# Decode attention with grouped K/V heads: the first K block is loaded ahead of wq and x, and transposed ahead of the q projection

## Chip, cores, metric

One core of a Trainium2 chip (trn2), the other cores idle. The time is that of one execution on the device, in microseconds (us); most executions of one kernel agree within 0.3%. Runs are called fast or slow by their time against the fastest of the same kernel (slow is over 1.5% longer), and only fast runs are compared. The span in a profile is some 1.8 us shorter than the time.

## The reference

```python
B, Sq, D = 8, 4, 512
Hq, Hkv, Sk, Dh = 32, 8, 2048, 128        # bfloat16 throughout

q = (x @ wq).reshape(B, Sq, Hq, Dh).transpose(0, 2, 1, 3)
k = repeat(k_cache, 4, axis=1);  v = repeat(v_cache, 4, axis=1)
scores = einsum("bhqd,bhkd->bhqk", q, k) * Dh ** -0.5
o = einsum("bhqk,bhkd->bhqd", softmax(scores), v)
out = o.transpose(0, 2, 1, 3).reshape(B, Sq, Hq * Dh) @ wo
```

K and V are 33.5 MB each, wq and wo 4.2 MB each: 75.5 MB to read, for little arithmetic.

## The kernel before

The work is 32 units (4 pairs of K/V heads x 8 batches). A unit needs one K block and one V block of 1 MB each. All loads go out on one queue, in a fixed order, as buffers come free (7 for K, 6 for V):

```python
nc.sync.dma_start(wq_sb[:, :, :], wq.rearrange("(p r) n -> p r n", r=R))   # 4 MB
nc.sync.dma_start(x_sb[:, :], x.flatten_outer_dims())                       # 32 KB
loads = []
for u in range(NU + KA):                       # NU = 32 units, KA = 4
    if u < NU:
        loads.append(("k", u))
    if u >= KA - 1 and u - KA + 1 < NU:
        loads.append(("v", u - KA + 1))
    ...                                        # parts of wo at the end
load_ready(0, 0)                               # as many as there are buffers for
```

Then come x's transposes, the q projection (128 matmuls `psq`), the spreading of q into block-diagonal form (`pse`, `q_bd`), and the loop. A step of the loop is half a unit: K is turned by PE transposes in two parts (`kp`), evicted to `kt`, scores, exp, and, six steps behind, values and norms:

```python
for step in range(-L - 1, NH):                 # L = 6, NH = 64
    i, j = step + L + 1, step + L
    if i < NH:
        transpose_part(i, 0)                   # 4 transposes, 1 eviction
    if 0 <= j < NH:
        scores(j)
    if i < NH:
        transpose_part(i, 1)
    ...                                        # norms, values, finish of `step`
    load_ready(min((i + 1) // 2, NU), max((step + 1) // 2, 0))
```

After the loop 8 projection matmuls, the last permutation of the output and the last 32 projection matmuls remain. A free buffer is not all that a load waits for: it also waits for the eighth load before it to land (in the trace of before, the ninth load waited 8.6 us for wq).

The softmax here doesn't subtract the row's maximum and nothing guards it: scores larger than these inputs give would overflow.

## Time and profile before

| | before |
|---|---|
| time, median of 3 runs | 190.12 us (190.0 to 193.26) |
| the profiled run: time; span | 190.41 us; 188.6 us |
| read from HBM | 75.53 MB |
| rate once running | 424 GB/s |
| busy: PE, DVE, ACT | 82%, 60%, 46% |
| x landed; scores of unit 0 began | 13.58; 23.51 us |
| first V load that waited long for its buffer (block 6), issued | 39.58 us |
| last wait for wo ended; end | 181.98; 188.6 us |

How to read it: the row `GB/s` of the page gives the rate in 40 slices of the span, and whether the stream of loads is ever interrupted. The chain of waits goes back from the last instruction; a load in it has length "issue to landing", which is mostly standing in line when the line is long. The timeline of the issuing queue (`SPq`) tells when a load was put in line. The row of the granted clock, `PEclk`: `9` or 1.00 is full speed.

### The profile page before, as it was taken

To read this page: it belongs to the slowest core of one execution; us is meant where nothing else is said; L and a number is where in the kernel's file an instruction comes from. 1 tells how busy PE (TensorE), PEld (TensorE's weight loads), DVE (VectorE), ACT (ScalarE), POOL (GpSimd) and SP (SyncE) were. 2 spreads that over 40 slices of the span, in tenths; PEclk is the share of its full clock that TensorE was granted. 3 is DMA by queue.
4 is the path that set the end of the run, shared out by engine and by line. 5 is a ranking of instruction groups with operands and counts; after the bars stand their busy time and mean duration, and the time that the engine had idled before them with its cause. 6 is when DMAs were issued, how large, how long until landed. Compare 5 with 4: busy or idle time off the path is not lost.

```text
span 188.6 us, 6460 instructions
## 1 busy us (share of the span) xinstructions
PE 154.3 (82%) x2892; PEld 139.7 (74%) x2892; DVE 113.7 (60%) x220; ACT 86.3 (46%) x170; POOL 1.1 (1%) x8
## 2 busy tenths in 40 slices
PE   0009887899999999999888789998886899899783
PEld 0008677699999898898788788887776788787572
DVE  6401754577777677767766567676665677663420
ACT  2003456665655666446554354555554555542000
POOL 2000000000000000000000000000000000000000
PEclk9999999999999999999999999999999999999999
DMA  6999999999999999999999999999999999999950
GB/s 222 445 389 429 424 427 424 424 424 429 422 419 429 424 419 420 433 424 419 422 429 426 426 424 419 433 419 422 431 417 429 422 424 431 415 425 425 414 205 9
DMA packets 10539, 75.97 MB, mean 403 GB/s; under 512 B 1200, under 2 KB 1296, under 8 KB 1936
## 3 DMA queue, kind: packets, MB, share of 16 engines
q1 hardware_dynamic: 10464, 75.55, 95.7%
q8 instruction: 22, 0.36, 0.7%
q14 instruction: 5, 0.04, 0.1%
q10 hardware_dynamic: 48, 0.02, 0.0%
HBM read 75.53 MB, written 0.03 MB: 401 GB/s over the span
## 4 chain that ended last, share of the span: by engine, by line
DMA 80%; PE 12%; ACT 3%; DVE 2%; issue 1%; SPq 0%; DVEq 0%
DMA k_sb<-in_k_cache_dram 64%; DMA wo_sb<-in_wo_dram 9%; DMA x_sb<-in_x_dram 7%; PE kp L200 4%; PE s_ps L218 2%; PE psq L162 2%; PE out_ps L310 2%; ACT kt L205 2%; DVE kt L207 1%; PE o_ps L242 1%; ACT probs L228 1%; DVE q_bd L186 1%; PE pse L177 1%; PE l_ps L256 0%; ACT q_bd L186 0%
## 5 line engine op out<-in xcount | busy, mean ns | idle before, releaser
L200 PE MATMUL kp<-ident,k_sb 128*128 128x128 f32 x512 | 80.9, 284 | 9.3 <-DMA k_sb<-in_k_cache_dram 9.1
L207 DVE COPY kt<-kp 128x1024 bf16<-128x1024 bf16 x96 | 65.4, 684 | 25.4 <-PE kp L200 24.8
L228 ACT ACTIVATE probs<-s_ps 64x256 bf16<-64x256 f32 x128 | 48.4, 378 | 67.1 <-PE s_ps L218 66.4
L200 PEld LDWEIGHTS kp<-ident,k_sb 128*128 128x128 f32 x512 | 55.2, 142 | 10.6 <-issue 10.1
L218 PE MATMUL s_ps<-q_bd,kt 128*128 128x64 bf16 x1024 | 42.4, 194 | 3.1 <-ACT kt L205 2.6
L218 PEld LDWEIGHTS <-kt 128*128 128x128 bf16 x1024 | 39.8, 98 | 4.8 <-ACT kt L205 3.1
L242 PEld LDWEIGHTS <-v_sb 128*128 128x128 bf16 x1024 | 34.4, 96 | 9.3 <-DMA v_sb<-in_v_cache_dram 1.9
L264 DVE TENSOR_REDUCE l_sb<-l_ps 128x32 f32<-128x512 f32 x32 | 22.1, 692 | 23.5 <-PE l_ps L256 23.5
L242 PE MATMUL o_ps<-probs,v_sb 128*128 128x32 bf16 x1024 | 35.1, 176 | 0.9 <-DMA v_sb<-in_v_cache_dram 0.9
L205 ACT COPY kt<-kp 128x1024 bf16<-128x1024 bf16 x32 | 32.4, 1012 | 0.8
L256 PE MATMUL l_ps<-probs,ones 128*128 128x512 bf16 x64 | 19.1, 379 | 0.0
L268 DVE RECIPROCAL r_sb<-l_sb 128x32 f32<-128x32 f32 x32 | 11.3, 353 | 1.1
L153 PE MATMUL xtp<-ident,x_sb 32*128 32x32 bf16 x4 | 0.5, 191 | 13.9 <-DMA x_sb<-in_x_dram 13.6
L153 PEld LDWEIGHTS <-x_sb 32*128 32x128 bf16 x4 | 0.3, 114 | 13.9 <-DMA x_sb<-in_x_dram 13.6
L169 ACT ACTIVATE qT_all<-psq 128x256 bf16<-128x256 f32 x4 | 1.5, 385 | 15.0 <-PE psq L162 15.0
L310 PE MATMUL out_ps<-wo_sb,oP 128*32 128x256 bf16 x64 | 7.6, 272 | 0.8 <-DMA wo_sb<-in_wo_dram 0.8
L310 PEld LDWEIGHTS <-oP 128*32 128x32 bf16 x64 | 6.1, 96 | 1.5 <-issue 0.7
L363 ACT CAST out_sb<-out_ps 32x256 bf16<-32x256 f32 x1 | 0.4, 362 | 14.5 <-PE out_ps L310 14.5
L273 DVE TENSOR_TENSOR oT_all<-o_ps,r_sb 128x32 bf16<-128x32 f32 x32 | 5.8, 182 | 1.7 <-PE o_ps L242 1.5
L256 PEld LDWEIGHTS <-ones 128*128 128x128 bf16 x64 | 6.0, 98 | 0.8 <-issue 0.4
L186 DVE CAST q_bd<-pse 64x512 bf16<-64x512 f32 x4 | 2.6, 682 | 4.7 <-PE pse L177 4.7
L156 DVE COPY xT_sb<-xtp 128x32 bf16<-128x32 bf16 x4 | 0.5, 170 | 7.1 <-PE xtp L153 7.1
(23 smaller groups left out, 34.4 us busy)
## 6 DMA issues: line engine op xcount, KB each, us to landing
k_sb<-in_k_cache_dram SPq DMA_DIRECT2D x32, 1024.0 KB, 20.2
v_sb<-in_v_cache_dram SPq DMA_DIRECT2D x32, 1024.0 KB, 20.1
wq_sb<-in_wq_dram SPq DMA_DIRECT2D x1, 4096.0 KB, 12.6
wo_sb<-in_wo_dram SPq DMA_DIRECT2D x2, 1024.0 KB, 18.5
wo_sb<-in_wo_dram SPq DMA_DIRECT2D x3, 512.0 KB, 17.6
wo_sb<-in_wo_dram SPq DMA_DIRECT2D x2, 256.0 KB, 13.2
x_sb<-in_x_dram SPq DMA_DIRECT2D x1, 32.0 KB, 12.4
out_dram<-out_sb SPq DMA_DIRECT2D x1, 16.0 KB, 1.4
```

The lines of the kernel that those rows point to most:

```text
L186: (nc.scalar.copy if g else nc.vector.tensor_copy)(out=q_bd[rows, p, :, :, g, :], in_=pse[rows, :, :, :])
L200: nc.tensor.transpose(kp[:, j, :], k4[:, w : w + 128], ident4[:, :])
L205: nc.scalar.copy(out=kt2, in_=kp2)
L207: nc.vector.tensor_copy(out=kt2, in_=kp2)
L218: nc.tensor.matmul(s_ps[:, 2 * j : 2 * j + 2, :], lhsT=k_t[:, j % (HC // 4), :, e], rhs=q_bd[:, p, e, b, :, :], start=(e == 0), stop=(e == 1),
L228: nc.scalar.activation(out=pr[rows, hf * HC : (hf + 1) * HC, cols], in_=s_ps[rows, :, cols], func=EXP)
L242: nc.tensor.matmul(o_ps[u][:, :], lhsT=vs[u][:, cc, :], rhs=pr[:, cc, :], start=(cc == 0), stop=(cc == C - 1),)
L256: nc.tensor.matmul(l_ps[:, :, :], lhsT=ones[:, :], rhs=pr[:, c : c + LC, :], start=(c == 0), stop=(c + LC == C),)
L264: nc.vector.tensor_reduce(out=l_sb[:, :], in_=l_ps[:, :, :].rearrange("d c q -> d q c"), axis=AX, op=ADD)
L268: nc.vector.reciprocal(r_sb[:, :], l_sb[:, :])
L273: nc.vector.tensor_tensor(out=oT_all[:, p * HP : (p + 1) * HP, b, :], in0=o_ps[u][:, :].rearrange("d (h s) -> d h s", h=HP), in1=r_sbs[u][ ...
L310: nc.tensor.matmul(out_ps[half][:, :], lhsT=oP[p][:, r, :], rhs=wo_sb[:, p, r, half * DH : (half + 1) * DH], start=(p == 0 and r == 0), st ...
```

## The change

Its intent: PE sat idle until x arrived at 13.6 us, since wq and x are first in line. With K block 0 ahead of them, its 16 transposes can fill that idle time, and the scores can follow the q projection at once.

```diff
+    load_k(0)
     nc.sync.dma_start(wq_sb[:, :, :], wq.rearrange("(p r) n -> p r n", r=R))
     nc.sync.dma_start(x_sb[:, :], x.flatten_outer_dims())
     loads = []
     for u in range(NU + KA):
-        if u < NU:
+        if 0 < u < NU:
             loads.append(("k", u))
...
+    (kt and transpose_part are moved up to here, unchanged)
+    for i in range(2):
+        for part in range(2):
+            transpose_part(i, part)
     for r in range(R):
         xtp = psum_o.tile([128, T], BF16, tag="o", name="xtp")
...
     for step in range(-L - 1, NH):
         i, j = step + L + 1, step + L
-        if i < NH:
+        if 1 < i < NH:
             transpose_part(i, 0)
         if 0 <= j < NH:
             scores(j)
-        if i < NH:
+        if 1 < i < NH:
             transpose_part(i, 1)
```

More of the change, by code (lines that the diff above doesn't have):

```diff
@@ L149, with transpose_part @@
         nc.vector.memset(t[:, :, :], 0.0)
+    kt = {}
+    def transpose_part(i, part):
+        u, hf = divmod(i, 2)
+        c0 = hf * HC + part * (HC // 2)
+        kp = psum_k.tile([128, HC // 4, 128], FP32, tag="k", name="kp")
+        k4 = ks[u][:, :, :].rearrange("s c d -> s (c d)").bitcast(FP32)
+        for j in range(HC // 4):
+            w = (c0 // 2 + j) * 128
+            nc.tensor.transpose(kp[:, j, :], k4[:, w : w + 128], ident4[:, :])
+        kp2 = kp[:, :, :].rearrange("k j s -> k (j s)").bitcast(BF16)
+        k_t = ktpool.tile([128, HC // 4, 128, 2], BF16, tag="kt", name="kt")
+        kt2 = k_t[:, :, :, :].rearrange("k j s e -> k (j s e)")
+        if part == 1 and hf == 1:
+            nc.scalar.copy(out=kt2, in_=kp2)
+        else:
+            nc.vector.tensor_copy(out=kt2, in_=kp2)
+        kt[(i, part)] = k_t
+    for i in range(2):
+        for part in range(2):
+            transpose_part(i, part)
     for r in range(R):
@@ L190 @@
     wo_sb = wpool.tile([128, G2, WR, D], BF16, tag="w", name="wo_sb")
-    kt = {}
-    def transpose_part(i, part):
-        u, hf = divmod(i, 2)
-        c0 = hf * HC + part * (HC // 2)
-        kp = psum_k.tile([128, HC // 4, 128], FP32, tag="k", name="kp")
-        k4 = ks[u][:, :, :].rearrange("s c d -> s (c d)").bitcast(FP32)
-        for j in range(HC // 4):
-            w = (c0 // 2 + j) * 128
-            nc.tensor.transpose(kp[:, j, :], k4[:, w : w + 128], ident4[:, :])
-        kp2 = kp[:, :, :].rearrange("k j s -> k (j s)").bitcast(BF16)
-        k_t = ktpool.tile([128, HC // 4, 128, 2], BF16, tag="kt", name="kt")
-        kt2 = k_t[:, :, :, :].rearrange("k j s e -> k (j s e)")
-        if part == 1 and hf == 1:
-            nc.scalar.copy(out=kt2, in_=kp2)
-        else:
-            nc.vector.tensor_copy(out=kt2, in_=kp2)
-        kt[(i, part)] = k_t
     def scores(i):
```

## The prediction

> **What bounds the kernel now.** I read the page's slices first, then the windows by stage, then the chain that ended last, and then the timeline of the start and of the DMA-issuing queue. The slices of the page:
>
> ```profile
> PE   0009887899999999999888789998886899899783
> DMA  6999999999999999999999999999999999999950
> GB/s 222 445 389 429 424 427 424 424 424 429 422 419 429 424 419 420 433 424 419 422 429 426 426 424 419 433 419 422 431 417 429 422 424 431 415 425 425 414 205 9
> HBM read 75.53 MB, written 0.03 MB: 401 GB/s over the span
> ```
>
> The DMA row reads 9 from the second slice to the 38th. The rate settles at about 424 GB/s and stays there; only the first slice and the last two are low. The kernel must read 75.53 MB, and 75.53 MB / 424 GB/s = 178.1 us, of a span of 188.6 us. The other 10.5 us are the ramp at the start (some 2 us until the first bytes flow, plus a slow first slice) and the work after the last weights land. PE shows 9 in many slices as well, so I checked whether it or the stream sets the pace where both are full:
>
> ```profile
> 38.00:44.00 6.00, 6.00 (x125) 5.68 (x123) 4.60 (x11) 3.51 (x8) 0.00 (x0) 1.00 1.01 423
> 60.00:165.00 105.00, 93.62 (x1818) 86.19 (x1814) 71.97 (x137) 54.89 (x109) 0.00 (x0) 1.00 1.01 424
> ```
>
> In these window rows (length, busy PE, PEld, DVE, ACT, POOL, granted clock, DMA share, GB/s) PE is full between 38 and 44 us, catching up from its late start, yet the stream still moves 423 GB/s. So even where PE is behind, the stream does not slow. The chain that ended last (start, length, what):
>
> ```profile
> 1.18 12.40 DMA x_sb<-in_x_dram
> ...
> 14.55 3.57 PE psq L162 x126
> ...
> 21.15 2.56 PE kp L200 x12
> ...
> 43.70 0.33 SPq L103
> ...
> 44.08 19.80 DMA k_sb<-in_k_cache_dram
> ...
> 165.09 16.89 DMA wo_sb<-in_wo_dram
> ...
> 182.02 3.67 PE out_ps L310 x32
> ...
> 185.71 0.36 ACT out_sb L363
> ```
>
> The trap is its first 43.7 us. It runs through the load of x, the q projection, the transposes and the compute behind them, up to a V load that is issued at 43.70. Taken literally, everything that starts the compute earlier would end the kernel earlier. But the link from 44.08 to 63.88 is a 1 MB block that took 19.8 us to land; at 424 GB/s one takes 1.049 / 424 = 2.47 us. It spent 17.3 us in line behind other blocks. What counts is whether the line ever runs empty. The issuing queue answers that:
>
> ```profile
> 1.65 2.05 SPq L93 DMA_DIRECT2D k_sb<-in_k_cache_dram  x4
> ...
> 13.38 0.33 SPq L103 DMA_DIRECT2D v_sb<-in_v_cache_dram  x1
> ...
> 24.84 0.33 SPq L93 DMA_DIRECT2D k_sb<-in_k_cache_dram  x1
> ...
> 33.97 0.33 SPq L93 DMA_DIRECT2D k_sb<-in_k_cache_dram  x1
> 39.58 0.33 SPq L103 DMA_DIRECT2D v_sb<-in_v_cache_dram  x1
> ```
>
> The longest gap there after the start, from 33.97 to 39.58, is a V load that waits for its buffer, which PE releases late. By 39.58 the slices have moved (222+445+389+429+424+427+424+424) x 4.715 us = 15.01 MB by 37.7 us, and 1.9 us x 424 = 0.79 MB more: 15.8 MB. Less wq and x (4.22 MB) that is 11 blocks; 16 K and V blocks had been issued. Five were still in line, 12.3 us of transfer. That is the reserve at its thinnest.
>
> **What the Trainium skill says.** "DMA: Bandwidth & Descriptors", section "Bandwidth", gives 425 GB/s for a 16 MB load to 128 partitions on one core, and 435 as the fabric's ceiling; this trace's 424 agrees, so the stream has no speed left to gain. The same page, "Queues, rings and completion order", says that each of the 16 engines consumes its ring's descriptors in order. The trace agrees: x, 32 KB, issued at 1.18 behind 4 MB of wq, lands 12.40 us later, after wq (waited for until 13.38). So K block 0 placed first delays wq and x by its own transfer time. "Perfetto Trace Analysis", section "Identifying the Most-Contended Engine", says to improve the most-contended engine first; here that is the DMA, and the change takes no byte from it.
>
> **The change part by part.** The same 75.53 MB, instructions and buffers remain; the built order confirms that each engine keeps its instructions but for place (one kt copy of the first block is still on ACT, three on DVE).
>
> (a) K block 0 goes first. It lands at an estimated 4.5 us (first bytes at about 1.8, plus 2.47, plus a little). wq and x land 2.47 us later: x at 13.58 + 2.47 = 16.05 us.
>
> (b) The 16 transposes of block 0 leave the place after the q projection. By the rows
>
> ```profile
> 20.95 2.76 PE L200 MATMUL kp<-ident,k_sb 128*128 128x128 f32 x12
> 22.04 0.69 DVE L207 COPY kt<-kp 128x1024 bf16<-128x1024 bf16 x1 [0.17 <-PE kp L200]
> 25.17 1.01 ACT L205 COPY kt<-kp 128x1024 bf16<-128x1024 bf16 x1
> ```
>
> the first 12 cost 2.56 us of the chain, the last four 0.48. They move to about 4.5 to 8.5 us, where PE has nothing to do. DVE is clearing probs until 6.94 us, so the first copy comes then: 6.94 + 3 x 0.69 = 9.0 us for the three, ACT's by about 9.2, all before x lands. Three PSUM buffers mean that the fourth group waits for the first copy; that is hidden too.
>
> (c) The q path shifts whole by 2.47 us. The first scores needed q and kt at 23.51. Now they need no kt copy, but their PSUM buffer waits for ACT's copy of the third q_bd part, which ended at about 21.27 + 0.60 = 21.87 and now ends at 24.3: scores 0 start about 0.8 us later. Scores 1 no longer wait for ACT's 1.01 us copy: they end at about 26.1 instead of 26.65. Net, the compute is about 0.5 us ahead (0.3 to 1.0) once it is under way: some 3 us of transposes removed against 2.47 us of later data.
>
> (d) That half microsecond meets the 12.3 us reserve and ends there. The K load issued at 24.84 waited 0.7 us for block 0's transposes; this goes away, and is worth nothing, as it stood in line anyway. The chain's last part, wo landing at 181.98, then 3.67 of projection, 0.36 of copy and about 2.5 of storing, is set by the stream's end, which is set by bytes and start. Sum on the path that ends the kernel: 0 us from the compute. The only direct handle is the ramp: wq comes in 32 KB runs per partition and moved 180 and 255 GB/s in the windows to 2.0 and to 4.7 us; K has 8 KB runs. If the engines fill sooner with those, 0 to 0.5 us is gained; I take 0.1.
>
> **The rivals.** First, the chain taken literally: the compute starts earlier and all moves up by (c), about 0.5 us, at the most by the 3.04 us of removed transposes if x were not delayed: 189.6, or 187.1. For it: the chain's first 43.7 us, the 7.4 us in which V loads waited for PE. Against it: the unbroken 424 GB/s. Even this is at most 1.6%.
>
> Second, the delayed x hurts: q arrives 2.47 us later, V buffers come free later, the stream starves. For it: the 5.61 us gap in issuing. Against it: five blocks in line; the release would have to slip 12 us. Even if nothing were gained by (b), it slips 2.5. Time: unchanged; if it did reach the end, 192.6.
>
> Third, eight transfers may be outstanding before the next issue (the ninth waited for wq until 13.38). Now the ninth waits for K block 0 and goes at about 5 us; the tenth waits for wq, until about 15.8. Six K and V blocks (6.3 MB, 14.8 us) are in line then: no gap.
>
> Fourth, the 16 DMA engines don't finish together: the rate falls through 307, 244, 205 and 158 GB/s from 179 to 183 us. Another start may shift which engine ends last, by some tenths either way. I expect this to be larger than any effect of the compute.
>
> **Range and chances.** Center 190.12 - 0.1 = 190.0 us. Runs of before spread 190.0 to 190.12 with one of 193.26; with some tenths for the ramp and the engines' uneven end, 189.3 to 190.8 should hold it 8 times in 10. Faster by 2% means below 186.3, which needs more than every rival that helps gives: 1%. Slower by 2%, above 193.9, needs a starved stream or slow runs: 1.5%. The rest is within 2%.
>
> **What would show it right or wrong.** Right: DMA at 9 from the second slice and about 424 GB/s; xtp beginning at about 16 us; kp between 4.5 and 8.5; first scores at 24 to 24.6; the wo landing within 0.6 us of 181.98; the tail unchanged at 6.6 us. The chain may name other lines in its first part without the end moving. Wrong: a dip of the rate between 15 and 50 us (a starved queue), a wo landing over 1 us earlier (the compute did set the end, or the ramp cost more than I read), or a tail longer than 7 us.

## The result, and the profile after

The changed kernel took 190.1 us (median of 4 runs, 189.96 to 190.4) against 190.11 for the kernel before: ratio 1.0001, 95% interval 0.9984 to 1.0019. A ratio here is the mean time of one kernel's fast runs over that of the other's fast runs of the same rounds, so not quite the ratio of the medians.

The slices of the page after (tenths of PE's granted clock, DMA share, rate):

```profile
span 188.3 us, 6428 instructions
...
PEclk9985869999999999999999999999999699999999
DMA  6999999999999999999999999999999999999950
GB/s 251 425 438 393 418 430 426 423 428 425 419 425 421 426 421 423 430 419 423 431 421 421 430 423 421 425 426 425 423 421 428 425 426 423 426 424 416 422 207 10
```

From the second slice on the stream is as unbroken as before, at the same rate. Counted packet by packet from the two traces, it is 0.09 MB, or 0.2 us of transfer, ahead of before at 20 us, at 60 and at 150, and 0.08 MB at 178. That is most of the 0.30 us by which the last wait for wo ends earlier here (181.68 against 181.98), but the profile of before is of an execution that took 190.41 us, 0.3 more than the median, so the two traces alone don't show that the change brought it.

The granted clock seems to dip early in this kernel and not in the kernel before. The clock records of the trace of before begin at 23.94 us, those of this one at 9.50. Before the first record, transposes start 213 ns apart in both traces, as they do in stretches recorded at half speed; at recorded full speed it is 109 to 120. So in that execution the kernel before, too, ran its transposes from 20.95 us on at half speed.

The chain that ended last (start, length, what):

```profile
1.65 14.00 DMA x_sb<-in_x_dram
...
16.62 3.55 PE psq L185 x126
...
23.54 1.01 PE s_ps L222 x16
24.55 0.91 PE kp L161 x4
...
43.54 0.33 SPq L103
...
43.92 19.61 DMA k_sb<-in_k_cache_dram
...
164.40 17.27 DMA wo_sb<-in_wo_dram
...
181.72 3.67 PE out_ps L314 x32
...
185.41 0.36 ACT out_sb L367
```

The first part of the chain is built differently: the 2.56 us of transposes behind the q projection are gone, x lands 2.07 us later (15.65 against 13.58). From 43.5 us on it is the same chain within some tenths, and the tail after the last wait is 6.6 us in both (188.3 - 181.68, 188.6 - 181.98). The timeline after, for the moved transposes and the V load that waited until 39.58 before:

```profile
5.66 3.65 PE L161 MATMUL kp<-ident,k_sb 128*128 128x128 f32 x16 [5.66 <-DMA k_sb<-in_k_cache_dram]
...
39.42 0.33 SPq L103 DMA_DIRECT2D v_sb<-in_v_cache_dram  x1
```

The transposes did move into idle time, and by the time it asks for the next V block the compute is 0.16 us ahead of that one trace of before (against another trace of the same start it is behind; see the section on PE's clock). The change works as built; it just does so where no microsecond counts.

### The profile page after: what moved, and what is told of

Same layout as the page of the kernel before. It is cut to its first block, busy times and chain, and to the rows that moved or that the text cites. A ratio compares the mean times of both kernels' runs of the same rounds, so it can differ in the third digit from the quotient of the medians.

```text
span 188.3 us, 6428 instructions
## 1 busy us (share of the span) xinstructions
PE 154.9 (82%) x2861; PEld 141.9 (75%) x2892; DVE 113.3 (60%) x220; ACT 86.3 (46%) x170; POOL 1.1 (1%) x8
## 4 chain that ended last, share of the span: by engine, by line
DMA 81%; PE 12%; ACT 3%; DVE 2%; issue 1%; SPq 1%; DVEq 0%
DMA k_sb<-in_k_cache_dram 64%; DMA wo_sb<-in_wo_dram 9%; DMA x_sb<-in_x_dram 7%; PE kp L161 3%; PE s_ps L222 3%; PE psq L185 2%; PE out_ps L314 2%; DVE kt L168 1%; ACT kt L166 1%; PE o_ps L246 1%; DVE q_bd L209 1%; ACT q_bd L209 1%; ACT probs L232 1%; PE l_ps L260 0%; PE pse L200 0%
## 5 line engine op out<-in xcount | busy, mean ns | idle before, releaser
L161 PE MATMUL kp<-ident,k_sb 128*128 128x128 f32 x512 | 83.1, 290 | 13.4 <-DMA k_sb<-in_k_cache_dram 13.4
L161 PEld LDWEIGHTS kp<-ident,k_sb 128*128 128x128 f32 x512 | 56.7, 146 | 14.4 <-issue 14.1
L222 PE MATMUL s_ps<-q_bd,kt 128*128 128x64 bf16 x1024 | 43.3, 195 | 3.1 <-ACT kt L166 1.9
L222 PEld LDWEIGHTS <-kt 128*128 128x128 bf16 x1024 | 40.7, 100 | 4.9 <-ACT kt L166 2.2
L260 PE MATMUL l_ps<-probs,ones 128*128 128x512 bf16 x33 | 12.4, 380 | 1.5
```

The lines of the kernel that those rows point to most:

```text
L161: nc.tensor.transpose(kp[:, j, :], k4[:, w : w + 128], ident4[:, :])
L222: nc.tensor.matmul(s_ps[:, 2 * j : 2 * j + 2, :], lhsT=k_t[:, j % (HC // 4), :, e], rhs=q_bd[:, p, e, b, :, :], start=(e == 0), stop=(e == 1),
L260: nc.tensor.matmul(l_ps[:, :, :], lhsT=ones[:, :], rhs=pr[:, c : c + LC, :], start=(c == 0), stop=(c + LC == C),)
```

## Experiments

The theory: the stream of loads sets the end; a compute that starts earlier or later only changes how long blocks stand in line, until the line runs empty. Rival A: the compute's start is on the path, and the change shows nothing because later x and earlier transposes cancel. That rival is serious: the two terms are nearly equal (2.07 us lost, 2.56 us gained). Twelve kernels were run, in three groups, each group on one chip together with runs of the kernel before.

### The two halves of the change, alone

`e1_load_first`: only the order of loads changes; the transposes stay behind the q projection.

```diff
+    load_k(0)
     nc.sync.dma_start(wq_sb[:, :, :], ...)
...
-        if u < NU:
+        if 0 < u < NU:
```

> Only the load order changes: K block 0 ahead of wq and x, its transposes stay behind the q projection. Theory (the stream of loads sets the end, a later compute is absorbed by the blocks in line): x lands at about 15.65 us as in the changed kernel, scores 0 start about 2.1 us later than before (25.6 instead of 23.5), the V load that waited until 39.58 goes at about 41.7, the rate stays at 424 GB/s, time 190.1 (ratio 1.000 +- 0.002). Rival A (the compute's start is on the path, and the change showed nothing because later x and earlier transposes cancel): 190.1 + 2.1 = 192.2, ratio 1.011.

Measured: 189.98 us (fast runs 189.83 to 190.16), ratio 0.9986 (0.9973 to 0.9999). The V load went at 40.30, only 0.7 us later than in the trace of before and not 2.1: in this run the 12 transposes behind q took 1.47 us rather than 2.76 (see the clock below). Against a trace of the same start without the edit in which they took 1.47 us too (`e7_one_block_less`, V load at 38.13) the delay is 2.2 us, as expected. Which of the two the timed runs of before had isn't known, so as a test against rival A this run is weaker than planned, but what delay there was did not show.

`e2_transposes_first`: only the order of the compute changes; block 0 then lands at 15.5 us, and the q projection stands behind its transposes.

```diff
+    for i in range(2):
+        for part in range(2):
+            transpose_part(i, part)
     for r in range(R):
         xtp = psum_o.tile(...)
...                                            # and taken out of the loop, as in the changed kernel
```

> Only the compute order changes: block 0's 16 transposes run ahead of the q projection, the load order is that of before, so that block 0 lands at about 15.9 us, after wq and x. Theory: x waits behind transposes on PE until about 19.2 us, scores 0 start at about 27 us, 3.5 us later than before; time 190.1 (ratio 1.000 +- 0.002). Rival A: 190.1 + 3.5 = 193.6, ratio 1.018.

Measured: 190.11 us, ratio 0.9995 (0.9981 to 1.0008). The V load:

```profile
42.57 0.33 SPq L103 DMA_DIRECT2D v_sb<-in_v_cache_dram  x1
```

That is 3.0 us later than in the trace of before. Rival A would have 3.0 us more; nothing was lost. Two halves that would have to cancel are each worth nothing alone: rival A falls.

`e3_after_again`: the changed kernel once more, same chip.

> The changed kernel again in more rounds, on the chip of the other runs. Both theories: 190.1, ratio 1.000 +- 0.002. Its profile shows whether the granted clock falls to about 0.5 between 13 and 19 us again (if the drop comes from the early PE work with the pause after it) and whether the stream is ahead by a few tenths at its end.

Measured: 190.05 us median; one run of the six, the profiled one, took 765.58 us and left a profile that says nothing of the kernel. The five others took 189.96 to 190.10; ratio of the fast runs 0.9988 (0.9975 to 1.0002). The question of the clock was left to the next run.

### The lost lead: PE's clock

`e4_warm`: filler matmuls between block 0's transposes and x's.

```diff
             transpose_part(i, part)
+    warm = psum_o.tile([128, 128], FP32, tag="o", name="warm")
+    for n in range(80):
+        nc.tensor.matmul(warm[:, :], lhsT=ident[:, :], rhs=ones[:, :],
+                         start=(n == 0), stop=(n == 79))
```

> The changed kernel with 80 filler matmuls 128x128 (results unused) between the first block's transposes and the transposes of x, so that PE does not pause between 9 and 15.7 us. If the drop of the granted clock to 0.5 at 13 to 19 and 23 to 26.6 us comes from the pause, it goes away, scores 0 take 0.65 us instead of 1.01, the groups of transposes 0.48 instead of 0.91, and the V load of 43.54 goes about 1 us earlier (the lead that the prediction had sized at 0.5). Theory: time still 190.1 (ratio 1.000 +- 0.002), as this lead meets blocks in line. Rival A: 1 us faster, ratio 0.995.

Measured: 190.0 us, ratio 0.9987 (0.9975 to 0.9999), but the drop did not go away. The fillers cut PE's pause before x from 6.4 to 1.3 us, and the granted clock still dropped, a little later. Windows of this run (length, busy PE, PEld, DVE, ACT, POOL, granted clock, DMA share, GB/s):

```profile
17.00:19.00 2.00, 2.00 (x83) 2.00 (x80) 0.00 (x0) 0.77 (x2) 0.00 (x0) 0.58 1.01 414
19.00:21.00 2.00, 1.95 (x47) 1.43 (x44) 0.40 (x1) 0.77 (x2) 0.00 (x0) 0.57 1.01 426
...
25.00:27.00 2.00, 2.00 (x23) 1.94 (x22) 0.69 (x1) 0.96 (x3) 0.00 (x0) 0.50 1.00 422
```

Scores 0 did take 0.68 us instead of 1.01, but the next two groups of transposes were slow again, and the V load went at 39.54: no lead. In the clock records this drop lasts from 17.32 to 20.73 us, in the middle of the q projection's back-to-back matmuls. A drop there doesn't have to start there: the changes of the clock in one trace lie multiples of 3.41 us apart (in the changed kernel at 9.50, 12.91, 19.74, 23.15 and 26.56), and 17.32 is the first such moment after the short pause, from 14.43 to 15.70. That this pause was enough fits; no run varied it alone, so the cause is not shown. Because the V load did not move, this run says nothing more on rival A.

PE's speed in the first 25 us differs between runs of one program. This shows when the kernel before is set against a later run that has the same program up to this point (`e7_one_block_less` below, which differs first at V block 15). The 12 transposes behind q in the kernel before, and in that run:

```profile
20.95 2.76 PE L200 MATMUL kp<-ident,k_sb 128*128 128x128 f32 x12
```

```profile
20.34 1.47 PE L203 MATMUL kp<-ident,k_sb 128*128 128x128 f32 x12
```

Both profiles show a granted clock of 1.00 there, yet one took almost twice as long. The clock records tell why: they begin at 23.94 us in the kernel before and at 18.55 in the later run, so that the first transposes came before the rise to full speed (213 ns apart) and the second after it (109 ns apart). The later run's V load went at 38.13 and not 39.58. A lead of 0.16 or 0.5 us is thus smaller than the 1.45 us by which one program varies from run to run; against the later run the changed kernel is 1.3 us behind. Whether the change makes the compute earlier at all isn't shown.

### How much delay the line absorbs

`e5_late2` and `e6_late5`: the kernel before with 2 and 5 extra passes of the q projection; results unchanged, no byte more.

```diff
-        for h in range(HP):
+        for h in [h for h in range(HP) for _ in range(2 + 1)]:     # 5 + 1
```

> The kernel before with the q projection computed three times (two extra passes of 128 matmuls, 3.8 us each by the row of the q projection): the whole compute starts 7.6 us later, no byte more. Theory: less than the reserve of about 12 us, so time 190.1 (ratio 1.000 +- 0.003), the rate flat at 424 GB/s. Rival A (the start of the compute is on the path): 197.7, ratio 1.04.

> The same with five extra passes: 19 us later. Theory: this exceeds the reserve (12.3 us by counting blocks in line; about 11.5 us by an estimate that steps through issue limits, buffers and 2.47 us a block), so the stream runs empty for the rest: a dip of the rate between 35 and 60 us and 190.1 + 7.5 = 197.6 (6 to 9 us longer, ratio 1.03 to 1.05). Rival A: 190.1 + 19 = 209. Rival B (compute has enough slack to make it up later): 190.1.

Measured: 191.96 us (ratio 1.0096, 1.0079 to 1.0113) and 207.46 us (1.0901, 1.0884 to 1.0919). Both miss what I expected. First, the passes delayed more than planned: 128 matmuls took about 3.6 us, and after the first 219 and then after every 128 PE stood still, mostly for 1.7 to 2.7 us, for which the profile shows no wait. A packet of 16 KB on the queue named "instruction" begins within 0.9 us of each of these stops (at 19.45 and 25.76 us in `e5_late2`, where PE stopped at 19.89 and 25.39) and ends before PE goes on. Only the last stop of `e6_late5` took 0.2 us; its packet came 2.4 us ahead of it, when hardly a load was left in line. That PE waits there for its next instructions is likely; no run tested it. The V load went at 50.44 and 65.99, 10.9 and 26.4 us later, not 7.6 and 19. Second, the reserve is smaller than the 12.3 us of blocks in line. Take the time gained from the delay: 10.86 - (191.96 - 190.21) = 9.1; 26.41 - (207.46 - 190.21) = 9.2. Two delays, one reserve: between the two, each microsecond of delay cost one, as PE cannot make up bytes that were not moved, and read back to no cost that gives 9.1 us. (That is counted from the V load at 39.58; put without a baseline, this load could go as late as 48.7 us.)

What the missing 3.2 us can be, the run with the emptied line suggests (windows of `e6_late5`, same columns):

```profile
38.00:40.00 2.00, 0.00 (x0) 0.00 (x0) 0.00 (x0) 0.00 (x0) 0.00 (x0) 0.50 0.72 299
40.00:42.00 2.00, 1.87 (x71) 1.86 (x70) 0.00 (x0) 0.00 (x0) 0.00 (x0) 0.50 0.14 49
...
51.00:52.00 1.00, 0.89 (x14) 0.75 (x12) 0.32 (x2) 0.96 (x3) 0.00 (x0) 1.00 0.00 0
52.00:53.00 1.00, 0.36 (x9) 0.36 (x10) 0.38 (x1) 0.59 (x1) 0.00 (x0) 1.00 0.70 115
53.00:54.00 1.00, 1.00 (x18) 0.99 (x16) 0.44 (x1) 0.76 (x2) 0.00 (x0) 1.00 0.88 369
```

The line does not empty at once: the rate falls over some 3 us while the busy share of the DMA engines falls with it (0.72, then 0.14): some have finished their share while others still work. And a load put in an empty line at 51.25 brings no byte until after 52; the shortest from issue to landing among this run's K loads is 4.7 us, of which 2.47 is transfer. So, as an estimate, a block must be in line about 2.2 us before it is needed. That the uneven end takes the rest, about 1 us, is argued and not measured. The 9.1 us itself doesn't rest on this split.

`e9_late1`: one extra pass, within that reserve.

> The kernel before with one extra pass of the q projection. In the two runs with two and five extra passes, the V load that waits for its buffer went 10.9 and 26.4 us later than in the kernel before, and the time grew by 1.8 and 17.2 us: both give a reserve of 9.1 us after which each further microsecond of delay costs one. One pass should delay by about 5 us (half of 10.9), within that reserve: 190.1, ratio 1.000 +- 0.002. If the cost is instead in proportion to the delay (rival A in a weak form, 1.8/10.9), 190.9, ratio 1.004.

Measured: 190.09 us (190.07 to 190.40 over 4 runs) with the V load at 44.85, 5.3 us late. The runs of before on this chip scattered, so the ratio of 0.9975 (0.9925 to 1.0025) can't tell 1.000 from 1.002; but all four runs lie at the time that the kernel before has on every chip, and 0.8 us more would be outside of them. With the 3.0 us of `e2_transposes_first` that makes two delays under 9.1 us that cost nothing. The cost is not in proportion to the delay: there is a threshold.

`e10_late2_v8`: the late kernel with two extra passes, with eight V buffers instead of six.

```diff
-    VB = 6
+    VB = 8
-        if step == NH - 1 - 2 * VB:
+        if step == NH - 1 - 12:
```

> The kernel with two extra passes (191.96, ratio 1.0096) with eight V buffers instead of six, so that the V loads that waited for PE at 50.44 us and after it can go two blocks earlier. If its 1.8 us come from the line of loads running empty behind those waits, they go away: 190.1 to 190.4, ratio 1.000 to 1.003, and the dip of the rate between 50 and 60 us is gone. If they come from the late compute itself, the ratio stays at 1.01.

Measured: 190.30 us (190.18 to 190.73), against 191.96 with six buffers; the ratio, again with the scattered runs of before, 0.9986 (0.9935 to 1.0037), keeps clear of 1.0096. The rate where it fell with six buffers, and with eight:

```profile
50.00:54.00 4.00, 3.95 (x83) 3.71 (x81) 3.07 (x6) 2.42 (x5) 0.00 (x0) 1.00 0.96 377
54.00:60.00 6.00, 5.95 (x123) 5.69 (x123) 4.55 (x9) 3.35 (x8) 0.00 (x0) 1.00 0.97 356
```

```profile
50.00:54.00 4.00, 4.00 (x84) 3.71 (x82) 2.95 (x7) 2.41 (x6) 0.00 (x0) 1.00 1.01 426
54.00:60.00 6.00, 6.00 (x124) 5.68 (x123) 4.60 (x10) 3.80 (x8) 0.00 (x0) 1.00 1.02 427
```

The compute starts at least as late (K block 7's load, which waits for block 0's transposes, went at 37.34 us, against 35.71 with six buffers), and the 1.8 us are gone. What cost time was the empty line and not the late compute. (Eight V buffers without the delay were not run; before's line never ran empty, so nothing suggests a gain of their own.)

### The stream itself

`e7_one_block_less`: V block 15 isn't loaded, block 14 is used twice; the result is wrong.

```diff
 def load_v(u):
+        if u == 15:
+            vs[u] = vs[u - 1]
+            return
```

> The kernel before without the load of V block 15 (block 14 is used twice, wrong result on purpose): all compute remains, the stream is 1.049 MB shorter. Theory: the stream sets the end, so 2.47 us less: 187.6, ratio 0.987. Rival A (the compute's chain sets the end): 190.1, ratio 1.000.

Measured: 187.74 us, ratio 0.9869 (0.9856 to 0.9881): 2.47 us less for 1.049 MB less, one block's transfer at 424 GB/s. All compute is still there. The last wait for wo ended at 179.36 instead of 181.98, with the same tail behind it:

```profile
179.40 3.67 PE out_ps L313 x32
```

This is the most direct evidence that the stream sets the end.

### The ramp at the start

`e12_wq_quarters`: the kernel before with wq in four loads.

```diff
-    nc.sync.dma_start(wq_sb[:, :, :], wq.rearrange("(p r) n -> p r n", r=R))
+    for r in range(R):
+        nc.sync.dma_start(wq_sb[:, r, :],
+                          wq.rearrange("(p r) n -> p r n", r=R)[:, r, :])
```

> The kernel before with wq loaded in four transfers of 8 KB runs per partition instead of one of 32 KB runs. The three kernels with K block 0 ahead of wq read 0.9986 to 0.9988, the one without 0.9995. If that 0.1% is the ramp, because engines fill sooner with 8 KB runs (the prediction's term of 0 to 0.5 us), this kernel shows it too: ratio 0.998 to 0.999. If not, 1.000 or, as three more of the eight outstanding transfers are spent at the start, no worse than 1.001.

Measured: 189.82 us, ratio 0.9969 (0.9916 to 1.0022). Unclear: of its fast runs four lie at 189.71 to 189.82, below the lowest run of before in that group (190.02), one at 190.75. In its trace the wait for wo ended at 181.41. That the first bytes come faster in 8 KB runs fits this run and the times of the three kernels with block 0 first in the first group (0.9986, 0.9987, 0.9988); the first comparison of the changed kernel, 1.0001, doesn't show it, and neither do the traces taken together. By 20 us this run's stream was 0.08 MB ahead of before and the changed kernel's 0.09, but those of `e1_load_first` and `e11_after_wo2`, which have block 0 first too, only 0.03 and 0.02. An effect of the start of 0.1 to 0.2% is possible, not shown.

### A version that is faster

`e8_wo2_halves`: what is left after the stream is the tail. wo's third part is loaded in halves, and the first half's 8 matmuls run ahead of the last permutation.

```diff
-            load_wo(2, 0, WR)
+            load_wo(2, 0, 4)
+            load_wo(2, 4, 4)
...
+    project(2, 0, 4)
     to_wo_rows(3)
-    project(2, 0, WR)
+    project(2, 4, 4)
```

> A try at what is left, the 6.6 us after the last wait: the load of wo's third part is split in two halves of 0.5 MB, and the 8 matmuls of the first half run ahead of the last permutation, so that 24 and not 32 projection matmuls follow the wait at 181.98. Theory: 8 x 114 ns = 0.9 us less at most, if the first half lands about 1.2 us before the second: 189.2, ratio 0.995. Rival: the permutation on PE and DVE is delayed by as much, 190.1.

Measured: 189.79 us (median of all six; two were slow), ratio 0.9974 (0.9961 to 0.9987), a gain of about 0.5 us.

`e11_after_wo2`: the same on top of the changed kernel.

> The changed kernel together with the split of wo's third part, the one edit that was faster (0.9974 of before). The block-0-first kernels read 0.9986 to 0.9988. If both are real and independent, 0.996 to 0.9965 of before (189.4 to 189.5); if the start's part is nothing, 0.9974.

Measured: 189.75 us (median of all six; two were slow), ratio 0.9949 (0.9899 to 0.9999) against the scattered runs of before; its fast runs, 189.59 to 189.82, are those of the split alone (189.61 to 189.80 without the slow ones), so block 0 first adds nothing that shows. The end of its chain:

```profile
177.91 0.98 PE o_ps L246 x32
178.91 0.20 DVE oT_all L277
179.16 0.62 PE nat L289 x8
179.78 0.87 PE out_ps L314 x8
180.67 1.03 PE out_ps L314 x8
181.70 0.60 PE perm L304 x8
182.30 2.75 PE out_ps L314 x24
185.07 0.36 ACT out_sb L369
```

Only 24 matmuls follow the last permutation, but it now starts at 181.70 behind the 8 that were moved up. The tail is bound by PE from the last V block on, so 0.5 us by the ratio of the split alone, and not 0.9, were gained: part of the rival that I had named.

## Why the prediction was right

- The bound: right. A load less is worth its transfer time (2.47 us measured, 2.47 by 1.049 MB / 424 GB/s); compute that asks for the V load 0.7 to 5.3 us later costs nothing. This also means that the number 190.1 doesn't confirm the sum in (c): it would have come out the same with the compute 3 us later, as it did in `e2_transposes_first`.
- The trap in the chain's first 43.7 us: right. Its parts changed places, and the end stayed.
- (a) block 0's landing was estimated at 4.5 us; the load that waited for it went at 5.54. x was delayed by 2.07 us and not 2.47 (15.65 against the estimated 16.05).
- (b) right: the transposes ran from 5.66 to about 9.3 us in idle time; ACT's copy ended at 10.35 instead of 9.2, still 5 us before x.
- (c) mis-sized: scores 0 began at 23.54 (estimated 24.3, range 24 to 24.6), scores 1 ended at 26.31 (26.1), and the lead at the V load was 0.16 us instead of 0.5. PE's clock is not in the sum: the same four transposes took 0.48 us at full and 0.91 at half speed. The 2.56 us that the sum takes off were read from an execution at half speed; where the clock had risen in time, the 12 transposes took 1.47 us (`e7_one_block_less`), and by the same sum (an estimate: 1.47 + 0.48 us off, 2.07 to 2.47 on) there is no lead.
- (d) right in kind, mis-sized: the reserve is 9.1 us, not 12.3. I counted blocks in line, and left out some 3 us: by the estimate above, what a new load needs before and besides its transfer (about 2.2 us), and that the engines run dry one after another. For this change the V load went 0.16 us earlier in the one pair of traces, and even the second rival's 2.5 us were far from 9.1.
- The wait for a transposed block 0 at 24.84 went away: block 7's load went at 24.41, and the waits of K loads for transposes (1.0 us in the issuing queue before) are no longer in the list.
- The ramp, taken at 0.1 us: open. 0.0 by the first comparison, up to about 0.25 by the later ones, and no steady head start in the traces. The 180 GB/s that the prediction read for wq up to 2.0 us were a misreading: the window counts packets where they start, and wq's are 32 KB; of the load queue's bytes 0.03 MB had moved by then.
- The fourth rival: the uneven end of the engines is in every trace looked at, but that it moved anything isn't shown. The wait for wo ended 0.3 us earlier than in the profile of before; 0.2 us of that was there at 178 us, before the rate falls.

## What to carry to other kernels

A load in the chain of waits that took eight times its own transfer was standing in line; what comes before it in the chain is not a reason for the end, unless the line ran empty. Find the reserve before pulling compute forward: blocks in line when the longest gap in issuing ends, less what a new load needs before its first byte and what engines that finish unevenly may take (some 3 us together here). If the reserve is positive, look at bytes, at the ramp, and at what follows the last landing. And before a stage of a few microseconds is put into a sum, check at which clock it ran.

## What the Trainium skill lacked or had wrong

- "DMA: Bandwidth & Descriptors", section "Anatomy of one DMA — SWDGE (gpsimd) path", gives some 2.0 us of fixed cost for a DMA, fitted on that path. No run here used it; on the queue of this kernel (the SP queue) the shortest K load of the run with the emptied line took 4.7 us for a transfer of 2.47, so 2.2 us. The page doesn't say that the same time is to be taken off a queue's reserve, where by the estimate above it helped to turn 12.3 into 9.1 us.
- "DMA: Bandwidth & Descriptors", section "Latency and other measured facts", calls two of the 16 engines usually slower and ties that to another way of issuing. Here, without it, the engines run dry unevenly at the end of the stream: the rate fell from 412 to 158 GB/s between 178 and 183 us in the kernel before. Which engines are last I did not look up.
- "TensorE: Matmul & The Clock Gate", section "HAM oscillation — how this bites in real kernels", ties a lowered clock to pauses of PE of over 3.4 us. Here drops came with much shorter pauses: in `e4_warm` at 17.32 us after one of 1.3, in `e6_late5` at 22.80 after one of 1.7, in `e9_late1` at 22.77 after one of 1.7. All lie in or behind matmuls with only 32 moving columns; whether that matters wasn't tested.
- No page that I read says that a trace can lack clock records up to the first rise, or that a profile's clock then reads as full. Here the first record lay at 23.94 us in one trace and at 18.55 in another of the same start, and 12 transposes before and after it took 2.76 and 1.47 us at a shown clock of 1.00.
- PE's stops in the repeated q projection, mostly 1.7 to 2.7 us after every 128 matmuls with their 128 weight loads, came each with a 16 KB packet of the queue named "instruction". If they are waits for instructions, which is likely and not tested, the page that they belong to is "Runtime: NRT & Kernel Launch", section "Instruction fetch mechanics", which gives no length for such a stop.
